# Gate and up matmuls of a routed FFN: four batches of eight weight pieces, one per token tile, in place of eight batches of four

## The chip, the cores and the metric

One core of one Trainium2 chip. The time is device microseconds (us) of one execution; the kernel before takes 261.04 us (median of three runs, 260.71 to 261.38). The engines are called PE (TensorE), DVE (VectorE), ACT (ScalarE), POOL (GpSimd), and SP for the queue that issues nearly all DMAs.

## The reference, cut to what matters

Two branches over the same 2048 tokens of width 1024, mixed by a sigmoid gate per token. Branch A is linear attention. Branch B routes one single token through an FFN with 3584 hidden units and adds the result to that token's row.

```python
def reference(A_x, A_wqkv, A_wo, B_x, B_w_r, B_w_gate, B_w_up, B_w_down, gate_w):
    x = A_x
    g = _sigmoid((x * gate_w).sum(-1, keepdims=True))
    a = _A_ref(x, A_wqkv, A_wo)                 # linear attention, 32 heads
    b = _B_ref(x, B_w_r, B_w_gate, B_w_up, B_w_down)
    return g * a + (1 - g) * b
# in _B_ref, for the one token with the largest x @ w_r:
#   g = _silu(x_sel @ w_gate); u = x_sel @ w_up; y = (g * u) @ w_down
#   y = y * sigmoid(r_sel); that row of x gets y added
```

The FFN computes little, but 22 MB of weights have to come in. They are streamed while branch A's matmuls run.

## The kernel before

Branch A works through 16 token tiles of 128 tokens. A tile has four KV units and mostly one or two Q units of eight 128x512 matmuls each, and a kvacc of eight short matmuls. Every unit's result leaves one of four PSUM buffers through ACT and DVE (tiles pk, vt, pq_all). Between the units the loop takes FFN steps; a step computes one weight piece and asks for the piece that fits in the buffer it frees.

```python
FFN_PER_T = {6: (0, 4), 7: (4, 4), 8: (4, 4), 9: (4, 4), 10: (4, 2), 11: (2, 2), 12: (1, 2), 13: (1, 2), 14: (1, 2), 15: (1, 0)}
FFN_DEPTH = 9
...
# 46 pieces in this order: 8 gate, 8 up (512 KB each), 8 gate, 8 up (384 KB), 14 down (512 KB)
def compute(wt, half=half, w=w, wi=wi, c=c):          # a gate or up piece
    ...
    for j in range(4):                                # 32-column tiles, four at once
        pe.matmul(ps[32 * j : 32 * j + 32, 0:w], lhsT=xs_pad[:, c, :], rhs=wt[:, w * j : w * j + w],
                         start=(c == 0), stop=(c == KC - 1), tile_position=(0, 32 * j))
    ...                                               # after 8 pieces: silu, or h_bf; then hps and hcol
def compute(wt, i2=i2, k0=k0, dk=dk):                 # a down piece: two DVE multiply-adds
    ...
    dve.scalar_tensor_tensor(yacc[:], w, h1, yacc[:], op0=ALU.mult, op1=ALU.add)
    if i2 == 13:                                      # the last one: sum over partitions on PE (yps)
        ps = ps_ffn.tile([P, 256], F32, tag="f", name="yps")
        ...
def ffn_step(n):
    for _ in range(n):
        ...
        wt, comp = inflight.popleft()
        comp(wt)
        ffn_prefetch()                                # fills up to FFN_DEPTH loads in flight
...
for t in range(4, NT):
    for nb in range(4):
        unit_KV(t, nb)
        if nb == 1 and t > 4:
            unit_KVACC(t - 1)
        if nb == 1:
            ffn_step(FFN_PER_T.get(t, (0, 0))[0])     # first number: after the second KV unit
    ...                                               # Q units
    ffn_step(FFN_PER_T.get(t, (0, 0))[1])             # second number: at the end of the tile
```

`hps` are the few matmuls that turn h_bf into the columns hcol that the down pieces multiply by. The tile framework keeps the emitted order on an engine only roughly: it moves instructions that it thinks ready.

Of the kernel before, what the change touches and what calls it, by code (L numbers as in the profile page):

```python
# [29 lines left out]
LN1EPS = math.log1p(EPS)  # L30
N_WARM = 5
Q_PER_T = {4: 2, 5: 1, 6: 1, 7: 2, 8: 1, 9: 1, 10: 2, 11: 1, 12: 1, 13: 2, 14: 1, 15: 0}
FFN_PER_T = {6: (0, 4), 7: (4, 4), 8: (4, 4), 9: (4, 4), 10: (4, 2), 11: (2, 2), 12: (1, 2), 13: (1, 2), 14: (1, 2), 15: (1, 0)}
FFN_DEPTH = 9
NORM_PER_T = [2, 0, 0, 3, 3, 3, 3, 3, 3, 3, 3, 3, 3, 3, 3, 3]

# [2 lines left out]
def kernel(  # L39
# [198 lines left out]
    def unit_Q(g, j):  # L238
        ps = ps_work.tile([P, 512], F32, tag="w")
        for c in range(KC):  # L240
            pe.matmul(ps[:], lhsT=wq[:, c, g * P : (g + 1) * P], rhs=xT[:, c, 512 * j : 512 * j + 512],
                             start=(c == 0), stop=(c == KC - 1))
        phi_evac(ps[:], pq_all[:, g, 512 * j : 512 * j + 512])
# [76 lines left out]
    def gates():  # L320
        strict[0] = True
        act.activation(gate[:], gl[:], ACTF.Exp, scale=-1.0)
        dve.tensor_scalar_add(gate[:], gate[:], 1.0)
        strict[0] = False
        dve.reciprocal(gate[:], gate[:])
        dve.tensor_scalar(omg[:], gate[:], -1.0, 1.0, op0=ALU.mult, op1=ALU.add)
# [142 lines left out]
    def ffn_step(n):  # L469
        for _ in range(n):  # L470
            pend = ffn_state.pop("pending", None)
            if pend is not None:
                pend()
            if not inflight:
                return
            wt, comp = inflight.popleft()
            comp(wt)
            ffn_prefetch()
# [4 lines left out]
    for t in range(4, NT):  # L483
        for nb in range(4):
# [3 lines left out]
            if nb == 1:  # L488
                ffn_step(FFN_PER_T.get(t, (0, 0))[0])
        nq = Q_PER_T[t]  # L490
# [8 lines left out]
        if t == 12:  # L499
            gates()  # L500
        ffn_step(FFN_PER_T.get(t, (0, 0))[1])
    unit_Q(*q_units.popleft())
# [147 lines left out]
```

## Time and profile before

| | us |
|---|---|
| time, median of 3 | 261.04 |
| span in the profile | 259.4 |
| PE busy | 251.2 |
| first down-projection multiply-add (yacc) starts | 108.72 |
| last one starts | 151.32 |
| yps starts on PE | 156.80 |
| next KV matmul after yps and the kvacc of tile 14 | 161.31 |

Times inside a kernel are from the start of the span. PE is the bound nearly everywhere, so I read every change as a shift of one and the same matmul on PE. The last row is the best such mark: it is the first matmul behind everything that the change moves. The prediction shows the lines.

### The profile page before, as it was taken

What the parts mean: (1) busy time and instruction counts of PE and PEld (TensorE: products, weight loads), DVE (VectorE), ACT (ScalarE), POOL (GpSimd) and SP (SyncE); (2) the same over time, 40 slices, a digit from 0 to 9 for tenths busy, and PEclk for the clock granted to TensorE, in tenths of its full rate; (3) what the DMA queues carried; (4) which work ended last, traced back from release to release, by engine and by line L of the source; (5) the groups of instructions that cost most, each with busy time, mean ns of one, the idle gap of its engine ahead of it and who ended that gap; (6) DMA issues with size and microseconds to landing.
All of it is one profiled execution on the core that took longest, in us unless ns stands there. A gap on an engine that the chain in (4) does not pass through costs nothing.

```text
span 259.4 us, 3816 instructions
## 1 busy us (share of the span) xinstructions
PE 251.2 (97%) x1413; PEld 117.3 (45%) x1440; DVE 147.4 (57%) x241; ACT 126.0 (49%) x200; POOL 47.0 (18%) x99
## 2 busy tenths in 40 slices
PE   7999999999999999999999999999999999999994
PEld 3444455444444444444444444444444444444443
DVE  1265015223146317299999982378983779964433
ACT  1095324555354445535546455366899741342310
POOL 6000001010000000000000000105993029960000
PEclk9999999999999999999999999999999999999999
DMA  6999950008999999999990000390000373555222
GB/s 213 385 317 227 258 222 1 0 3 208 352 348 350 330 300 313 348 347 387 339 435 3 0 0 0 121 322 26 1 3 0 92 251 124 157 166 164 81 81 81
DMA packets 45433, 47.71 MB, mean 184 GB/s; under 512 B 16284, under 2 KB 33060, under 8 KB 45352
## 3 DMA queue, kind: packets, MB, share of 16 engines
q1 hardware_dynamic: 45128, 47.34, 57.7%
q8 instruction: 11, 0.18, 0.3%
q0 software_dynamic: 256, 0.14, 0.2%
q14 instruction: 6, 0.05, 0.1%
q10 hardware_dynamic: 32, 0.00, 0.0%
HBM read 39.86 MB, written 8.40 MB: 186 GB/s over the span
## 4 chain that ended last, share of the span: by engine, by line
PE 70%; DVE 14%; DMA 7%; issue 4%; SPq 3%; ACT 0%; POOLq 0%; DVEq 0%; POOL 0%
PE ps L75 62%; DVE yacc L75 10%; DMA wt<-in_B_w_gate_dram 3%; SPq L388 3%; DMA wt<-in_B_w_down_dram 3%; PE first L75 2%; PE kvacc L75 2%; DVE pk L75 1%; DVE pq_all L75 1%; PE pst L75 1%; PE warm_ps L75 1%; DVE xT L75 1%; PE dps L75 1%; DMA xsel<-in_A_x_dram 1%; PE rps L75 1%
## 5 line engine op out<-in xcount | busy, mean ns | idle before, releaser
L75 PE MATMUL ps<-wkv,xT 128*128 128x512 bf16 x465 | 107.2, 379 | 1.5 <-DVE pk L75 0.5
L75 PEld LDWEIGHTS <-xT 128*128 128x128 bf16 x512 | 48.5, 98 | 60.8 <-issue 5.5
L75 PE MATMUL ps<-xT,wq 128*128 128x512 bf16 x251 | 58.4, 379 | 0.6 <-DVE pk L75 0.3
L75 PE MATMUL ps<-m_sb,pq_all 128*128 128x512 bf16 (+1 forms) x258 | 55.3, 372 | 0.3
L75 ACT ACTIVATE u<-ps 128x512 f32<-128x512 f32 x60 | 35.8, 596 | 40.7 <-PE ps L75 38.5
L75 ACT ACTIVATE e<-u 128x512 f32<-128x512 f32 x64 | 40.4, 631 | 1.7
L75 PEld LDWEIGHTS <-pq_all 128*128 128x128 bf16 x264 | 25.8, 98 | 29.8 <-issue 0.4
L75 PEld LDWEIGHTS <-wq 128*128 128x128 bf16 x256 | 24.8, 98 | 30.5 <-issue 1.4
L564 POOL TENSOR_TENSOR pq_all<-pq_all,rb 128x512 bf16<-128x512 bf16 x32 | 36.0, 1157 | 6.0 <-DVE rb L75 6.0
L75 ACT CAST vt<-ps 128x512 bf16<-128x512 f32 x32 | 18.8, 587 | 36.5 <-PE ps L75 35.3
L75 DVE SCALAR_TENSOR_TENSOR yacc<-wt,hcol,yacc 128x1024 f32<-128x1024 bf16 x27 | 34.6, 1281 | 0.5
L75 DVE SCALAR_TENSOR_TENSOR ot<-ps,gate,xg 128x512 bf16<-128x512 f32 (+1 forms) x33 | 24.1, 739 | 16.7 <-PE ps L75 15.0
L75 DVE SCALAR_TENSOR_TENSOR pq_all<-ps,e 128x512 bf16<-128x512 f32 x32 | 22.0, 687 | 19.2 <-ACT e L75 19.0
L75 DVE SCALAR_TENSOR_TENSOR pk<-ps,e 128x512 bf16<-128x512 f32 x28 | 19.2, 687 | 22.5 <-ACT e L75 22.5
L75 ACT ACTIVATE xg<-xt,omg 128x1024 f32<-128x1024 bf16 x16 | 18.2, 1147 | 25.9 <-DVE ot L75 25.9
L75 DVE STREAM_SHUFFLE rb<-rdp 128x512 f32<-128x512 f32 x32 | 22.8, 762 | 0.0
L213 POOL MEMSET vt<- 128x8 bf16 x16 | 1.9, 137 | 107.9 <-PE kvacc L75 107.9
L75 PEld LDWEIGHTS <-pk 128*128 128x128 bf16 x128 | 8.5, 98 | 3.3 <-issue 0.4
L75 PE MATMUL kvacc<-vt,pk 128*128 128x129 bf16 x128 | 9.7, 221 | 0.0
L75 ACT CAST m_sb<-ps 128x512 bf16<-128x512 f32 x16 | 9.3, 583 | 0.0
L75 DVE COPY xT<-pst 128x1024 bf16<-128x1024 bf16 x4 | 2.8, 691 | 10.2 <-PE pst L75 10.2
L75 PE MATMUL first<-wkv,xT 128*128 128x512 bf16 x31 | 7.7, 380 | 0.6 <-DVE xT L75 0.6
(96 smaller groups left out, 84.1 us busy)
## 6 DMA issues: line engine op xcount, KB each, us to landing
wt<-in_B_w_down_dram SPq DMA_DIRECT2D x14, 512.0 KB, 6.8
wt<-in_B_w_gate_dram SPq DMA_DIRECT2D x8, 512.0 KB, 8.3
wt<-in_B_w_up_dram SPq DMA_DIRECT2D x8, 512.0 KB, 8.8
xt<-xp SPq DMA_DIRECT2D x16, 256.0 KB, 2.7
out_dram<-ot SPq DMA_DIRECT2D x15, 256.0 KB, 2.0
wt<-in_B_w_gate_dram SPq DMA_DIRECT2D x8, 384.0 KB, 7.0
wt<-in_B_w_up_dram SPq DMA_DIRECT2D x8, 384.0 KB, 6.1
wkv<-in_A_wqkv_dram SPq DMA_DIRECT2D x8, 256.0 KB, 4.9
```

The source lines that it names most:

```text
L75: inst = fn(*a, **k)
L213: nc.gpsimd.memset(vt_t[t][:, :, 128:129], 1.0)
L388: ld = nc.sync.dma_start(out=wt[:, 0 : 4 * w].rearrange("p (j f) -> p j f", j=4), in_=wv[:, c, :].rearrange("p (j f) -> p j f", j=4)[:, :, ...
L564: nc.gpsimd.tensor_tensor(sl, sl, rb[:], op=ALU.mult)
```

## The change

The intent: entering and leaving the 32-column tiling costs PE something each time; half as many batches, half as many times. The pieces, their order, and the buffers stay.

```diff
-FFN_PER_T = {6: (0, 4), 7: (4, 4), 8: (4, 4), 9: (4, 4), 10: (4, 2), 11: (2, 2), 12: (1, 2), 13: (1, 2), 14: (1, 2), 15: (1, 0)}
+FFN_PER_T = {7: (8, 0), 8: (0, 8), 9: (0, 8), 10: (0, 8), 11: (2, 2), 12: (1, 2), 13: (1, 2), 14: (1, 2), 15: (1, 0)}
```

## The prediction

> **What bounds the kernel now.** I read the page first, then the matmul rows by shape, then the timelines of TensorE (PE) and VectorE (DVE) through the stretch that the change touches (60 to 165 us), then the chain of waits.
>
> ```profile
> span 259.4 us, 3816 instructions
> PE 251.2 (97%) x1413; PEld 117.3 (45%) x1440; DVE 147.4 (57%) x241; ACT 126.0 (49%) x200; POOL 47.0 (18%) x99
> PEclk9999999999999999999999999999999999999999
> ...
> L75 PE MATMUL ps<-wt,xs_pad 128*32 128x512 bf16 x64 | 4.4, 382 | 0.3 <-DMA wt<-in_B_w_gate_dram 0.3
> L75 PE MATMUL ps<-wt,xs_pad 128*32 128x384 bf16 x64 | 3.3, 329 | 0.0
> L75 DVE SCALAR_TENSOR_TENSOR yacc<-wt,hcol,yacc 128x1024 f32<-128x1024 bf16 x27 | 34.6, 1281 | 0.5
> ```
>
> PE is busy from 1.4 us to the end at full granted clock: any saving must be PE time, and any new PE wait is paid in full. The FFN gate and up matmuls that are regrouped are only 7.7 us of PE, 128 matmuls in 8 batches of 16.
>
> ```profile
> 67.05 1.89 PE L75 MATMUL ps<-xT,wq 128*128 128x512 bf16 x8
> 68.87 1.05 PE L75 MATMUL ps<-wt,xs_pad 128*32 128x512 bf16 x16
> 69.85 3.63 PE L75 MATMUL ps<-wkv,xT 128*128 128x512 bf16 x15
> 73.31 0.63 PE L75 MATMUL kvacc<-vt,pk 128*128 128x129 bf16 x8
> 73.88 0.83 PE L75 MATMUL ps<-wt,xs_pad 128*32 128x512 bf16 x12
> 75.03 0.40 PE L75 MATMUL ps<-wt,xs_pad 128*32 128x512 bf16 x4 [0.32 <-DMA wt<-in_B_w_gate_dram]
> 75.36 3.63 PE L75 MATMUL ps<-wkv,xT 128*128 128x512 bf16 x15
> ```
>
> Here one sees the price of a batch, and that the second batch already waits for its last weight piece (the eighth, landed at 74.98).
>
> ```profile
> 92.00:104.00 12.00, 11.79 (x88) 5.54 (x89) 5.63 (x7) 5.92 (x10) 0.14 (x1) 1.00 1.00 304
> 104.00:116.50 12.50, 12.39 (x88) 5.74 (x88) 7.69 (x9) 5.79 (x10) 0.13 (x1) 1.00 1.01 347
> 116.50:161.00 44.50, 43.96 (x230) 20.40 (x233) 39.05 (x45) 23.51 (x40) 0.84 (x3) 1.00 0.47 172
> ```
>
> The windows' columns are PE, weight loads, DVE, ACT, POOL, clock, DMA share, GB/s. DMA is full until 116; DVE is then nearly full (39.05 of 44.5) with the 28 multiply-adds of the down projection. That chain is the second thing to watch: it starts when the first down piece lands and ends at the small PE reduction yps.
>
> ```profile
> 108.72 0.75 DVE L75 TENSOR_SCALAR yacc<-wt,hcol 128x1024 f32<-128x1024 bf16 x1 [5.05 <-DMA wt<-in_B_w_down_dram]
> ...
> 151.32 1.27 DVE L75 SCALAR_TENSOR_TENSOR yacc<-wt,hcol,yacc 128x1024 f32<-128x1024 bf16 x1
> 152.52 0.69 DVE L75 SCALAR_TENSOR_TENSOR pq_all<-ps,e 128x512 bf16<-128x512 f32 x1
> ```
>
> DVE idles 5.05 us for the first down piece (landed at 108.59); the last multiply-add ends near 152.6. On PE's timeline yps comes 4.2 us later, so it finds its operand ready:
>
> ```profile
> 156.80 0.64 PE L75 MATMUL yps<-yacc,ones_f 128*32 128x256 f32 x8
> 157.37 3.63 PE L75 MATMUL ps<-wkv,xT 128*128 128x512 bf16 x16
> ```
>
> **What the Trainium skill says.** "TensorEngine Tiling (Array Packing)", Key Properties: changing the tiling mode drains TensorE. The trace agrees: into a 32-column batch the step from the last full-array matmul is 0.309 us where 0.216 is usual, out of it 0.312, then 0.227 once: 0.093 + 0.096 + 0.011 = 0.20 us for each batch. "DMA: Bandwidth & Descriptors", Anatomy of one DMA: about 2 us of a DMA are fixed, mostly completion. Here a 384 KB piece issued at 94.56 into a nearly empty queue landed at 98.76, 4.2 us, against 1.2 us a piece in a full stream. "TensorE: Matmul & The Clock Gate", the section on the array as 32x32 sub-arrays: VectorE is strict FIFO; so one late down piece holds all evacuations behind it, as the 5.1 us above show.
>
> **The change part by part.** Instructions, shapes and bytes stay; the loads keep their order and the nine buffers. Only the places change: gate in tile 7 after the second KV unit (before: half at the end of tile 6, half there), up at the end of tile 8, second gate at the end of 9, second up at the end of 10. Down pieces start in tile 11 (4, 3, 3, 3, 1 per tile) instead of tile 10. The order of instructions shows yps moved from the end of tile 14 to after the second KV unit of tile 15, and DVE runs of five multiply-adds where there were four.
>
> (1) Switches: 8 batches become 4, so 4 x 0.20 = 0.8 us less PE work.
>
> (2) Batch one gains nothing. It starts at 73.88 - 1.07 = 72.8 (the tile 6 batch is gone), and could end by 74.7, but piece eight lands at 74.98 whatever PE does (pieces are 1.5 us apart, issued beforehand). PE waits about 0.8 us more than its present 0.5 and reaches the next KV matmul at 75.36, as now. One switch of saving is lost; three remain, 0.6 us.
>
> (3) Later batches, by adding present distances. A unit of 8 matmuls is 8 x 0.2158 = 1.73 us, a kvacc 0.475. Up: 75.36 + 4 units = 82.28; tile 8 has 5 units and a kvacc, less 0.01 of switch, so 91.4; the batch is 8 x 0.216 + 0.20 = 1.92, to 93.3. Its pieces are all in by about 87.5. Second gate: 93.3 + 9.1 + hps 0.1 + two early KV matmuls 0.43 = about 103.0, to 104.55. Its pieces: eight buffers come free only from 91.9, the first load lands 4.2 us on (96.1), the seventh, the last this batch needs, 7.2 us later, 103.3; PE needs it near 104.2. No wait, or 0.2 us. Second up: 104.55 + 10.4 = 115.0; its last piece lands near 114.9 and is needed near 116.2. It ends at 116.5, where the present kernel is at 117.06 with the same work: 0.6 us ahead, as counted.
>
> (4) The down chain starts later. The first down piece now goes out behind the seven second-up pieces, in the burst that starts when the second gate frees its first buffer: 103.05 + 0.39 = 103.45. First landing 107.65; six more at 1.2 us and the 512 KB down piece at 1.36 give 116.2. In the present trace the corresponding eight landings took 9.8 us rather than 8.6 (98.76 to 108.59), so up to 117.5. I take 116.8, against 108.72 now: 8 us later. VectorE then waits for it with nothing else it may do.
>
> (5) DVE work from there to the last multiply-add. In the present stream a multiply-add takes 1.295 us when another follows, 1.20 when something else follows (the first, a tensor_scalar, 0.67); an evacuation (pk or pq_all) 0.60. New order: runs of 1, 1, 2, 5, 1, 5, 1, 4, 1, 1, 1, 4, 1 = 28: 0.67 + 1.2 + 2.5 + 6.45 + 1.2 + 6.45 + 1.2 + 5.15 + 3.6 + 5.15 + 1.2 = 34.8. Between them 15 evacuations, 9.0; h_bf, hcol and gate 0.9. Sum 44.7. It has no idle, since every operand is ready long before. End: 116.8 + 44.7 = 161.5.
>
> (6) PE reaches yps after 23 units (4+1, 5, 6, 5 and 2 of tiles 11 to 15), 5 kvaccs and hps: 116.5 + 39.7 + 2.4 + 0.1 = 158.7, if PSUM buffers never hold it. I checked each unit against the evacuation four units back. With DVE 8 us later but PE not, they mostly come 0.2 to 2 us in time, since VectorE no longer evacuates just behind each multiply-add run at the moment PE needs it. The present stream has some 1.3 us of such small waits (0.68 us step at 143.15 the largest), which mostly go. At the late edge of (4), one of 0.1 and an hps wait of up to 1 us come back.
>
> (7) So yps waits about 161.6 - 158.7 = 2.9 us, and the next KV matmul starts near 161.6 + 0.6 = 162.2. The same matmul, with the same work done, starts at 161.31 now. Net +0.9 us. From there on PE is the bound in both kernels, so the shift stays.
>
> Sum: -0.8 (switches) + 0.2 (batch one held to the same time) - 1.3 (PSUM waits gone) + 2.9 (new wait) - 0.1 (rounding) = +0.9 us.
>
> **The rivals.** (a) Only the switches count and everything else hides: 261.04 - 0.6 or -0.8 = 260.3. For it: PE is 97% busy. Against: DVE has 4 us of slack at yps and is moved by 8. (b) Bursts starve the weight stream: eight buffers come free at once, so DMA idles between bursts and both 384 KB batches wait. For it: margins of 1 us in (3), and the present kernel's 0.32 us wait; a 2 us slip in each would give about 264 to 265, since the down chain would slip by it too. Against: the full-stream spacing of 1.2 us. (c) The down chain's delay reaches the output: yps, then the scattered row write, then the final loads. The write lands near 164.7, and the first such load leaves at 164.95 today for want of PE memory release, so it should be hidden; otherwise 1 or 2 us. (d) The opposite, first down piece at 115, with yps 1.5 us earlier: 260.5.
>
> **Range and chances.** The central value is 261.04 + 0.9 = 261.9 us. The start of the down chain (116.2 to 117.5) gives 261.3 to 262.6; DMA jitter and rival (a) widen it to 260.6 to 263.4. Two per cent is 5.2 us; only a pile-up of (b) goes there: slower 0.02, faster 0.01, same 0.97.
>
> **What would show it.** In the new profile: four batches of 32 narrow matmuls; a wait of about 0.8 to 1.2 us for the gate DMA before 75.03 and a KV matmul at 75.36; the first yacc at 116.2 to 117.5 after a long DVE idle on the down DMA (over 4 us); VectorE without idle to about 161.5; yps near 161.6 with a wait of 2 to 3.5 us on yacc; the steps over 0.22 us between 120 and 153 mostly gone. I am wrong if yps doesn't wait, if a batch after the first waits more than 0.5 us for its weights, or if the offset at 161 is not the offset at the end.

## The result, and the profile after

264.46 us (median of 4 runs, 262.95 to 264.62) against 260.98 for the kernel before: ratio 1.0131, 95% interval 1.0085 to 1.0178. Ratios here are the mean time of one kernel's fast runs over the mean of the other's in the same rounds, so not quite the ratio of the medians. Slower, by less than 2%, and 1.1 us above the predicted range.

The run that was profiled is the fastest one. The head of its page:

```profile
span 261.2 us, 3845 instructions
PE 251.4 (96%) x1440; PEld 117.9 (45%) x1440; DVE 147.6 (56%) x241; ACT 126.1 (48%) x200; POOL 47.0 (18%) x99
```

Its PE timeline around the first and the third batch and around yps:

```profile
73.16 1.69 PE L75 MATMUL ps<-wt,xs_pad 128*32 128x512 bf16 x28
75.23 0.40 PE L75 MATMUL ps<-wt,xs_pad 128*32 128x512 bf16 x4 [0.38 <-DMA wt<-in_B_w_gate_dram]
75.57 3.63 PE L75 MATMUL ps<-wkv,xT 128*128 128x512 bf16 x16
...
103.27 1.32 PE L75 MATMUL ps<-wt,xs_pad 128*32 128x384 bf16 x28
105.01 0.35 PE L75 MATMUL ps<-wt,xs_pad 128*32 128x384 bf16 x4 [0.43 <-DMA wt<-in_B_w_gate_dram]
105.29 3.19 PE L75 MATMUL ps<-wkv,xT 128*128 128x512 bf16 x14
...
159.55 0.64 PE L75 MATMUL kvacc<-vt,pk 128*128 128x129 bf16 x8
162.53 0.64 PE L75 MATMUL yps<-yacc,ones_f 128*32 128x256 f32 x8 [2.34 <-DVE yacc L75]
163.10 3.63 PE L75 MATMUL ps<-wkv,xT 128*128 128x512 bf16 x16
```

The first batch still ends when its eighth piece comes. The third now waits too, for the last piece of the second gate. And yps, which had its operand 4 us early, waits 2.34 us. The DVE timeline shows why:

```profile
116.91 0.76 DVE L75 TENSOR_SCALAR yacc<-wt,hcol 128x1024 f32<-128x1024 bf16 x1 [6.40 <-DMA wt<-in_B_w_down_dram]
...
121.34 2.61 DVE L75 SCALAR_TENSOR_TENSOR yacc<-wt,hcol,yacc 128x1024 f32<-128x1024 bf16 x2 [0.82 <-DMA wt<-in_B_w_down_dram]
...
161.20 1.28 DVE L75 SCALAR_TENSOR_TENSOR yacc<-wt,hcol,yacc 128x1024 f32<-128x1024 bf16 x1
```

The down chain starts 8.2 us later than before, idles once more, and ends at 162.48. The mark on PE went from 161.31 to 163.10, 1.8 us later, and the last matmul of the kernel also starts 1.8 us later (255.81 and 257.62): nothing is added or given back behind it. Of the 1.8 us, 0.36 us are already there at 36 us (the router matmuls start at 36.06 before and 36.42 here), ahead of any changed instruction. So this fastest run shows about 1.4 us of real loss, where 0.9 was predicted. The other runs are 1.4 us and more slower than this one, and their results list something the fastest doesn't have: a mean granted clock of 0.991 to 0.993 in two of the four. (The granted clock is the share of the full TensorE clock that the profile records; 1 is full speed.)

### The profile page after: what moved, and what is told of

It reads as the page before. It is cut to its first block, busy times and chain, and to the rows that moved or that the text cites. A ratio compares the mean times of both kernels' runs of the same rounds, so it can differ in the third digit from the quotient of the medians.

```text
span 261.2 us, 3845 instructions
## 1 busy us (share of the span) xinstructions
PE 251.4 (96%) x1440; PEld 117.9 (45%) x1440; DVE 147.6 (56%) x241; ACT 126.1 (48%) x200; POOL 47.0 (18%) x99
```

## The experiments

Theory: the burst of eight frees the weight buffers late, so that the down chain starts late, and PE waits for its end at yps. Rivals: the later place of the down steps and of yps alone; the batches themselves waiting for weights; for the slow runs, the start of the kernel or chance. Every kernel gave the right result. All runs below were timed in five rounds against the kernel before, whose medians were 261.29, 261.28 and 261.51 us. The first two ran on one chip, the third on another.

**1. The changed kernel again.** No edit.

> The changed kernel itself, once more, for its spread and a second profile. Theory (late down chain): median 263 to 264.5 us; in the profile the first yacc starts at 116.5 to 118.5 us, VectorE is full to the last yacc 44.7 to 46 us later, and yps waits 2 to 4 us on yacc; the slower the run, the later the first yacc. Rival (the loss of the slow runs lies elsewhere, in the start or in the clock): the first yacc stays at 116.9 us and the extra time is before 60 us or after 165 us.

263.9 us (262.47 to 265.63), ratio 1.0102, interval 1.0068 to 1.0136. This profile is of a run of 264.84 us with clock 0.992. PE timeline, lines after the kvacc of tile 14:

```profile
162.82 0.83 PE L75 MATMUL yps<-yacc,ones_f 128*32 128x256 f32 x8 [2.33 <-DVE yacc L75]
163.58 5.07 PE L75 MATMUL ps<-wkv,xT 128*128 128x512 bf16 x16
```

yps waits as long as in the first profile, but the 16 KV matmuls behind it take 5.07 us instead of 3.63. Half of them start 0.427 us apart where 0.216 is usual. I took the busy times by stretches of 3.41 us, laid so that they meet the record of the clock (columns: stretch, length, PE, weight loads, DVE, ACT, POOL, clock, DMA share, GB/s):

```profile
159.71:163.12 3.41, 1.07 (x18) 0.63 (x16) 3.41 (x4) 1.23 (x2) 0.00 (x0) 1.00 0.00 0
163.12:166.53 3.41, 3.41 (x15) 1.03 (x8) 1.33 (x3) 0.00 (x0) 0.58 (x1) 0.50 0.01 1
166.53:169.95 3.42, 3.37 (x16) 1.57 (x16) 0.00 (x0) 1.18 (x2) 0.00 (x0) 1.00 0.16 13
```

The clock is at half for exactly one stretch (3.413 us in the record), the one that follows a stretch in which PE worked only 1.07 us. The first profile of the changed kernel, whose clock record has the same grid at another phase:

```profile
158.15:161.56 3.41, 2.04 (x16) 1.04 (x13) 3.37 (x4) 2.33 (x4) 0.00 (x0) 1.00 0.00 0
161.56:164.97 3.41, 2.44 (x17) 1.05 (x18) 2.60 (x4) 0.00 (x0) 0.57 (x1) 1.00 0.00 0
```

There the same wait lies across a boundary, no stretch is mostly idle, and the clock stays. So the prediction lacked a term, and the spread has a candidate: where the wait falls in a grid that the kernel doesn't control. The expectation that slower runs have a later first yacc was only partly met: it is 118.11 here, but its end (last yacc starts at 161.49) is only 0.3 us later than in the fast run.

**2. yps later on PE.** The last down piece and yps move from after the second KV unit of tile 15 to its end.

```diff
-... 14: (1, 2), 15: (1, 0)}
+... 14: (1, 2), 15: (0, 1)}
```

> The changed kernel with the last down piece and the yps reduction moved from after the second KV unit of tile 15 to the end of tile 15, so that PE has 3.45 us of KV matmuls to do before it needs the last yacc. All loads and batches stay. Theory (the only new loss is PE waiting for yacc at yps): 2.3 us less than the changed kernel's fastest run, so 260.3 to 261.0 us, and the spread of several us goes too, since a late chain hides. Rival (the batches themselves wait for weights, or the loss is elsewhere): 263 us or more, the wait moves rather than goes.

261.09 us (260.21 to 262.38), ratio 1.0003. Its PE timeline:

```profile
160.39 3.62 PE L75 MATMUL ps<-wkv,xT 128*128 128x512 bf16 x16
163.93 0.64 PE L75 MATMUL yps<-yacc,ones_f 128*32 128x256 f32 x8
```

The first yacc is as late as ever (118.18), but PE has work to do until the last one is done. 2.8 us come back, and no run is below a clock of 0.999; the median is just above the 260.3 to 261.0 us expected. A spread of 2 us stays, which the theory had expected to go.

**3. Eight batches at the later places.** This separates merging from moving. The down steps are exactly those of the changed kernel.

```diff
-FFN_PER_T = {7: (8, 0), 8: (0, 8), 9: (0, 8), 10: (0, 8), 11: (2, 2), ...}
+FFN_PER_T = {7: (4, 4), 8: (4, 4), 9: (4, 4), 10: (4, 4), 11: (2, 2), ...}
```

> Gate and up in eight batches of four again, but at the places of the changed kernel's later schedule (tiles 7 to 10, twice in each), with the down steps exactly as in the changed kernel (first at tile 11). Theory (the burst of eight frees buffers late, so the first down piece lands late): only four loads stand ahead of the first down piece, it lands near 111.5 us rather than 116.8, yps waits less than 0.5 us, time 260.7 to 261.6 us although four switches of 0.2 us come back. Rival (the later place of the down steps and of yps is what costs, not the merging): 263 us or more with a yps wait of over 2 us.

> The version with eight batches of four at the later places (nine buffers) again, for confirmation that it beats the kernel before: ratio 0.992 to 0.997, 259.5 to 260.4 us. It fails if the interval reaches 1.

259.9 us (ratio 0.9947, interval 0.9927 to 0.9966), and 260.13 when repeated (0.9945, 0.9929 to 0.9961). From the DVE and then the PE timeline of the first:

```profile
113.16 0.75 DVE L75 TENSOR_SCALAR yacc<-wt,hcol 128x1024 f32<-128x1024 bf16 x1 [2.60 <-DMA wt<-in_B_w_down_dram]
```

```profile
159.42 0.64 PE L75 MATMUL kvacc<-vt,pk 128*128 128x129 bf16 x8
159.99 0.64 PE L75 MATMUL yps<-yacc,ones_f 128*32 128x256 f32 x8
```

The first yacc comes 3.8 us earlier than in the changed kernel (I had expected 5), and yps doesn't wait. The time is below the 260.7 to 261.6 us expected. So it is the merging, not the later place. And this version beats the kernel before, with the same eight switches. Most of that 1.4 us can be seen in the starts of matmuls. Before, PE loses 0.49 us in the first batch to its last weight piece, and 1.3 us in ten small steps between 122 and 154 us while it waits for DVE to empty a PSUM buffer. Here the first batch doesn't wait, and from 122 us to yps there are three such steps, 0.43 us in all (none in the second profile); in return two later batches start 0.27 and 0.13 us late.

**4. Ten weight buffers.** The changed kernel with one more buffer, the most that fits. PE's order stays.

```diff
-FFN_DEPTH = 9
+FFN_DEPTH = 10
```

> The changed kernel with ten weight buffers in place of nine (there is room for no more); PE order unchanged. Every load moves one place forward in its burst, so the first down piece lands about 1.3 us earlier (115.5 us) and the second comes in the same burst, so that VectorE no longer idles 0.8 us between them. Theory: the yps wait falls by about 2 us, time 2 us below the changed kernel of the same call. Rival (buffers don't set it): no change.

260.85 us (259.3 to 261.6), 3 us below the changed kernel, where 2 had been expected. From the DVE and then the PE timeline:

```profile
115.90 0.75 DVE L75 TENSOR_SCALAR yacc<-wt,hcol 128x1024 f32<-128x1024 bf16 x1 [6.52 <-DMA wt<-in_B_w_down_dram]
```

```profile
159.96 0.64 PE L75 MATMUL yps<-yacc,ones_f 128*32 128x256 f32 x8
```

As expected the first piece is about 1 us earlier, the second comes in the same burst (landed at 117.1 instead of 121.24), the last yacc starts at 158.44, and yps at 159.96 doesn't wait. One buffer more removes the loss. But not by the loads alone: the chain ends 2.75 us earlier than in the first profile (159.73 and 162.48), of which 1.0 is the earlier start, 0.8 the missing idle, and the remaining 0.9 comes with DVE's order, which the framework changed too (one evacuation, 0.6 us, moved behind the last yacc).

**5. Filling the wait.** To see whether the idle PE causes the half clock: 20 matmuls on zeros, written to the yps buffer before yps overwrites it. (`strict` makes the framework keep the emitted order on PE.)

```diff
+                    strict[0] = True
+                    for _ in range(20):
+                        pe.matmul(ps[:], lhsT=warm_sb[:, 0:P], rhs=warm_sb[:, 0:256], start=True, stop=True)
+                    strict[0] = False
```

> The changed kernel with 20 matmuls of 128x256 on a tile of zeros (about 0.11 us each, 2.2 us together) put on PE between the kvacc of tile 14 and yps, that is, in the time in which PE only waits for yacc. They hide in the wait. Theory (an idle PE of 2.3 us there lets the granted clock fall to half for one window of 3.4 us, in about half of the runs): no run has a mean clock below 0.997 any more, the runs near 265 us vanish, median 263 to 263.5 us. Rival (the clock falls for another reason, chance or power): about half of the runs still show a clock of 0.991 to 0.993, median 263.9 us or, with the added work, more.

> The filled version (20 matmuls on zeros inside the yps wait) again, in the same call as the changed kernel. Theory: no run below a clock of 0.997, median 0.4 to 1 us below the changed kernel of this call, 263.0 to 263.7 us. Rival: some runs below 0.995, no difference.

> The changed kernel a third time, beside its filled version on the same chip. Theory: a mean clock of 0.991 to 0.993 in some of the six runs (it was so in 5 of 11), these 1.3 to 2 us slower than the others; median 263.5 to 264.5 us.

The first time 263.36 us. The second time, beside the changed kernel, 263.42 us (ratio 1.0066, interval 1.0048 to 1.0084), and the changed kernel 264.95 (1.0129, 1.0095 to 1.0162). So the gap is 1.5 us, where 0.4 to 1 had been expected, and the changed kernel was slower than the 263.5 to 264.5 expected; four of its six runs had the low clock. PE timeline of the first filled run:

```profile
159.95 2.35 PE L75 MATMUL yps<-warm_sb 128*128 128x256 bf16 x20
162.45 0.64 PE L75 MATMUL yps<-yacc,ones_f 128*32 128x256 f32 x8 [0.16 <-DVE yacc L75]
```

yps starts where it did, but PE was idle for only 0.16 us. None of the 12 filled runs has a clock below 0.998. Of the 17 runs of the changed kernel whose clock is known (5, 6 and 6; one of the first five isn't in the median above), 9 have 0.991 to 0.993; these take 265.20 us on average and the other eight 263.56. The 1.65 us between them is what the half-speed stretch shows in the first experiment: 16 KV matmuls in 163.58 to 168.49 instead of 3.45 us, 1.46 us, and 0.19 us on yps. (That the two agree to the digit is luck: the difference of the two groups has a standard error of 0.3 us.)

**6. A longer wait.** yps is forced ahead of the KV units of tile 15, so PE idles longer.

```diff
-... 14: (1, 2), 15: (1, 0)}
+... 14: (1, 3), 15: (0, 0)}
@@ before the yps matmuls (and taken back after the first KV unit of tile 15)
+                    strict[0] = True
```

> The changed kernel with yps forced ahead of the KV units of tile 15, which leaves the end of yacc where it is (near 162.5 us), so that PE idles about 6.2 us in place of 2.3. Theory: the half-speed window then comes in every run (mean clock 0.994 or less in all), and the time is about 263.5 + 3.9 (work no longer done in the wait) + 1.7 or more (half clock): 268.5 to 271 us. Rival (idle time has nothing to do with the clock): 267.4 us, clock 0.999 in most runs.

268.68 us, ratio 1.0282. All six runs have a clock of 0.985 to 0.994. Its stretches:

```profile
156.09:159.50 3.41, 0.90 (x10) 0.55 (x8) 3.34 (x3) 1.23 (x2) 0.00 (x0) 0.99 0.00 0
159.50:162.91 3.41, 0.07 (x4) 0.08 (x8) 3.24 (x4) 0.00 (x0) 0.00 (x0) 0.50 0.00 0
162.91:166.33 3.42, 3.42 (x14) 1.01 (x15) 0.48 (x1) 0.00 (x0) 0.57 (x1) 0.51 0.01 1
```

PE waits 5.79 us at yps; the half clock starts behind the first mostly idle stretch and ends behind the first busy one. Together with the filled version this makes the idle time the cause of the half clock: no wait, no drop; 2.3 us, a drop in about half of the runs; 5.8 us, in all.

The clock records of all 14 profiles also say how idle a stretch must be, and so why it is about half. Stretches of the grid with up to 1.40 us of PE work were followed by half clock (besides those above, one at the end of the kernel in each of eight profiles, with 0.49 to 1.40 us), and those with 1.42 us or more were not. (Some matmul records can be missing from a trace, so the limit is rough.) For a wait of 2.34 us to leave 1.4 us of work or less in one stretch of 3.41, at least 2.0 us of it must lie there. My estimate from these numbers is that a wait at a random place in the grid does so in 51% of runs; 9 of 17 did.

**7. Both repairs together, and more buffers with eight batches.** The first takes four batches, ten buffers, and yps at the end of tile 15; the second experiment 3 with ten buffers.

> Both repairs at once: four batches of eight, ten buffers, yps at the end of tile 15. Theory: no wait on yacc and no half clock in any run, four switches fewer; PE also doesn't wait for the second gate's pieces. Time 259.0 to 260.3 us, at or below the eight-batch version of the first call (259.9). Rival (the bursts cost more than the switches give): 260.5 us or more.

> Eight batches of four at the later places, with ten buffers. Theory: yps already doesn't wait there, so one more buffer hides: the same as the eight-batch version of the first call, 259.6 to 260.3 us. Rival (the buffers help by themselves): 259.3 us or less.

Both missed. The first gave 260.6 us (259.97 to 262.56), the second 260.99 where 259.6 to 260.3 had been expected. In the second profile the framework, given the tenth buffer, has put six multiply-adds ahead of the next pq_all on DVE, where there were five, the first yacc starts at 112.56, and eight PSUM steps are back between 134 and 157 us, 1.2 us in all, where the nine-buffer version had three. That the order did it rather than the buffers is argued, not tested. In the first, PE and then DVE show a new wait:

```profile
121.42 0.23 PE L75 MATMUL hps<-sel,h_bf 128*128 128x4 bf16 x3 [0.92 <-DVE h_bf L75]
```

```profile
116.43 0.75 DVE L75 TENSOR_SCALAR yacc<-wt,hcol 128x1024 f32<-128x1024 bf16 x1 [6.73 <-DMA wt<-in_B_w_down_dram]
...
120.81 0.55 DVE L75 TENSOR_TENSOR h_bf<-ps,sg 128x384 bf16<-128x384 f32 x1
```

DVE works in its fixed order. h_bf was ready for it at 116.4, when the second up batch ended, but two pq_all and three yacc stand ahead of it, and the first of these had waited for a DMA until just then, so that all of their work was still to do.

**8. h_bf ahead of the chain.** Four batches, ten buffers, late yps, and one dependence that only orders DVE (cut; another line keeps the h_bf instruction in `ffn_state`):

```diff
-                        dve.tensor_scalar(yacc[:], w, h1, None, op0=ALU.mult)
+                        first_y = dve.tensor_scalar(yacc[:], w, h1, None, op0=ALU.mult)
+                        tc.add_manual_dep(first_y.ins, ffn_state["h"].ins.name, NOSYNC, reason="h before the down chain")
```

> Four batches, ten buffers, yps at the end of tile 15, and on VectorE h_bf (and with it the two pq_all before it) put ahead of the first yacc, so that nothing that PE soon needs stands behind the wait for the first down piece. Theory (the profile of the version without it shows PE waiting 1.1 us at hps for h_bf, held behind yacc in VectorE's order): that wait goes, the time falls by about 1 us to 259.3 to 260.0 us and the spread narrows. Rival (the hps wait only moves to a later PSUM wait): 260.6 us as without it.

259.57 us (258.79 to 259.76), ratio 0.9927, interval 0.9913 to 0.9941. DVE timeline:

```profile
116.89 0.55 DVE L75 TENSOR_TENSOR h_bf<-ps,sg 128x384 bf16<-128x384 f32 x1
117.36 0.75 DVE L75 TENSOR_SCALAR yacc<-wt,hcol 128x1024 f32<-128x1024 bf16 x1
```

h_bf comes 3.9 us earlier, hps follows the kvacc without a wait, the first yacc no longer idles for its piece, and the runs lie within 1 us. This is the lowest median found, 1.9 us below the kernel before. But experiment 3's version, with all eight batches, was only 0.56 us above it in the same call (260.13; the intervals overlap), and the two differ in four things: batches, buffers, the place of yps, and DVE's order. So these runs don't show that fewer switches save time. Eight batches with the late yps and this order were not tried.

## Why the prediction was wrong, step by step

The mechanism was right and was named ahead: DMA holds the first down piece back, DVE is full from there, yps waits, and the shift stays to the end. Two sizes were short and one term was missing.

- Steps (1) and (2), the switches and the first batch: right in the main. The step into a batch is 0.309 us after as before; what four batches fewer save in time, no run isolates. The KV matmul behind the first batch starts at 75.57, which is 0.2 us later than before and less than the 0.36 us that this run had lost by 36 us. PE waited 0.56 us in that batch; the 0.8 to 1.2 us that was named doesn't fit step (2)'s own figures, which leave 0.66 (74.7 to 75.36).
- Step (3), the second gate's batch: too optimistic. Its last piece was to land at 103.3 us, from pieces 1.2 us apart. By the trace's record of landings the first one came at 95.97 (96.1 predicted), but the last at 104.97: in a burst two of the gaps were 1.9 and 2.15 us. So PE waited 0.60 us (0.753 us between the starts of two matmuls where 0.153 is usual), and everything behind it came later. More than 0.5 us here was one of the prediction's own signs of being wrong. This is rival (b), in small; that the median lies in its 264 to 265 us is luck, since it took 2 us in each of two batches, and the fourth batch didn't wait.
- Step (4), the start of the chain: 116.91 us in the fast run, 116.8 predicted. In two more profiles of the same kernel it was 118.11 and 117.87, outside the 116.2 to 117.5 that was given, so the close hit was partly luck.
- Step (5), "It has no idle, since every operand is ready long before": wrong by 0.82 us in the fast run. Only the first down piece was in the burst; the second had to wait for the next buffer and landed at 121.24. Otherwise the chain's length holds: 116.91 + 44.7 + 0.82 = 162.43, measured 162.48. (Its 6.45 and 5.15 us for runs of five and four don't follow from its 1.295 and 1.20, which give 6.38 and 5.09; the trace has 6.47 and 5.16.) In the other two profiles the chain starts about 1 us later and doesn't idle. Either way it ends at 162.5 to 162.8 rather than at 161.5.
- Step (6), PE at yps: 160.02 rather than 158.7. Of this, 0.2 us is the run's late start (the first batch's wait took up the rest of its 0.36), 0.5 had been added by the end of the third batch, and two PSUM waits, 0.29 and 0.36 us, are the rest. So the wait came out at 2.34 us rather than 2.9, while its end was later by 1 us.
- Step (7), the net: +0.9 predicted, +1.4 in the fastest run. This is the step that failed. It counted the wait at its length, as the first part had put it: "any new PE wait is paid in full". It is paid more than in full: the wait is long enough to halve the clock behind it, in 9 of 17 runs, at 1.65 us each, 0.9 us on average, as much as the whole predicted loss.

The sum over all 17 runs: mean 264.4 us, about 3.1 above the kernel before. 0.9 was predicted, 0.9 is the half clock, and some 1.3 is the later end of the chain and what the start and the DMA vary. Not settled: the eight runs at full clock still lie between 262.47 and 264.62 us, and only one of them was profiled. The four-batch versions 2, 4 and 7 scatter by 2 us too, the eight-batch ones and version 8 by 1 us, so I suspect the landings in a burst. The traces show that these vary: from the first to the third landing of the second-gate burst took 3.06 us in the first profile and 4.80 and 3.97 in the other two of this kernel, where 1.2 us a piece would be 2.4; in the burst behind it 3.28, 4.65 and 4.20. What holds the third piece back is open, and no run shows that this makes the spread of the whole time.

Rival (c), a delay through to the output, didn't occur: the shift is 1.8 us at 163 us and 1.8 us at the last matmul. In experiment 1's profile it does grow, from 2.3 us at the KV matmul behind yps (163.58) to 3.7 at the last matmul (259.55). That is the half clock, and it is the third of the prediction's signs: the offset at 161 is not the offset at the end.

## What to carry to other kernels

Work that frees several buffers at once also asks for several loads at once: look at the first load behind the burst, and at who needs it, before counting what the merging saves. On an engine that works in order, put what the critical engine needs next ahead of anything that may wait for a DMA. And price a wait on PE not only at its length: if it leaves most of a clock window empty, the matmuls behind it run at half speed for a while.

## What the Trainium skill lacked or had wrong

- "TensorE: Matmul & The Clock Gate", What's actually happening: it gives half clock after at least one idle window of about 3.4 us, on a free-running grid. The grid and the length agree (half clock for 3.413 us, at multiples of it). But the window needn't be wholly idle, and the page gives no threshold: 2.33 us of waiting, in a window in which PE was still busy 1.07 us, was followed by half clock, and so were windows with up to 1.40 us of work; windows with 1.42, 2.04 and 2.44 us were not. What the page's section on oscillation charges for a throttled stretch, half of its length, agrees: 1.65 us measured for 3.413.
- "TensorEngine Tiling (Array Packing)", Key Properties: it says that a change of mode drains the array, with no price. Here 0.09 us going in and 0.11 us coming out, 0.20 us for each batch.
- "DMA: Bandwidth & Descriptors", Anatomy of one DMA: 2 us of fixed cost and 436 GB/s would be 2.9 us (an estimate from the page's formula, which is fitted on the GpSimd path) for a 384 KB load. From the SP queue, with the queue run dry, it took 3.84 us (issued at 92.13, landed at 95.97), and in the burst of seven that began so the last landed 9.0 us after the first, where a full stream has 7.2.
